# Summing z in linear attention: VectorE pre-adds two of the five key tiles for pairs three to nine

## The chip, the cores and the metric

One core of one Trainium2 chip runs the kernel. The metric is device time in microseconds (us), the median of several runs; a profile of one execution comes with it.

## The reference

A linear attention with exponential features, then a two-layer network. What matters here is the attention, for 8 batches of 8 heads, 576 positions, 64 dimensions, 128 features:

```python
def phi(x):
    proj = np.einsum('bhsd,df->bhsf', x, w_phi)
    proj = proj - np.max(np.abs(proj), axis=-1, keepdims=True)
    return np.concatenate([np.exp(proj), np.exp(-proj)], axis=-1)
q_p, k_p = phi(q), phi(k)
kv = np.einsum('bhsf,bhsd->bhfd', k_p, v)
z = np.sum(k_p, axis=2)
num = np.einsum('bhsf,bhfd->bhsd', q_p, kv)
den = np.einsum('bhsf,bhf->bhs', q_p, z)[..., None] + 1e-06
attn = num / den
h = x @ w_in                       # x: attn as 4608 tokens of 512
out = (max(h, 0) + alpha * min(h, 0)) @ w_out
```

z is the sum of the key features over the 576 positions of one head.

## The kernel before, in words

The work is cut into 32 pairs of heads, numbered from i = 0. A pair's 576 key positions lie on the partitions as five tiles of positions: four of 128 in one buffer (`xk` in the profile, `c["x", 0]` in the code) and the last 64 in another (`k`, `c["x", 1]`), whose other 64 partitions are zero. Per pair, TensorE projects keys and queries (`pj`, `pl`, line 316; chunk 0 is four key tiles, chunk 1 is the fifth key tile and the queries), VectorE takes the row maximum `m` (line 320) and subtracts it (`t`, line 321), ScalarE takes the two exponentials (lines 334 and 329), TensorE sums z with a matrix of ones (`k_z`, line 374) and kv with v (`k_acc`, line 357), ScalarE copies both out (`ks`), TensorE turns them (`kt`) and the queries (`qt`), and then computes the denominators `d` (line 440) and the numerators `n` (line 422).

The reciprocal of the denominators takes a way round: ScalarE copies `d` to `ds`, SyncE's queue writes it as `d9`, VectorE inverts it (`r`, line 459, `invert`), SyncE writes it to memory (`rec_d`, line 462) and reads it back spread over partitions (`rr`, line 467), GpSimd multiplies `s` with it (line 472), and SyncE stores `x_d` (line 475).

Beside this, weights are decoded in blocks, two per visit: SyncE loads `raww` (line 167), ScalarE scales it (`aw`, line 176), VectorE splits it in four instructions (lines 184 to 187, `decode_split`), GpSimd adds (`aw`, line 192), ScalarE casts (`w`, line 127) and GpSimd takes the rest (`w`, line 131). From about 80 us on, the first layer of the network reads attention results back (`xr`, line 528, 1 MB), which ScalarE casts (`xh`) and GpSimd completes (`xl`, line 131).

What is done when is a hand-written list: each step of pair i has a place i + t in `places`, all steps are sorted by place, and TensorE, VectorE, ScalarE and SyncE carry out their own in that order. GpSimd's instructions are put in order by a scheduler. A visit, below, is one turn of this list, from the start of TensorE's sum of z to the next one; it is named by its start in the profile (34.15, 44.73, 55.30 and so on). In the visit that sums z of pair i, VectorE finishes chunk 1 of pair i + 1 and chunk 0 of pair i + 2.

z is formed in two ways. For pairs with i < ZP = 9, `k_sum` does nothing and `k_z` runs over all five tiles; from i = 9 on `k_sum` has VectorE add the five tiles into one in three steps, and `k_z` takes that one. For each tile `k_z` issues four matmuls (two heads, two signs), of 32 columns of ones each, which write four different quarters of the output's partitions; the profile counts two TensorE instructions for each.

Of the kernel before, what the change touches and what calls it, by code (L numbers as in the profile page):

```python
# [8 lines left out]
F32 = mybir.dt.float32  # L9
# [3 lines left out]
ALU = mybir.AluOpType  # L13
# [3 lines left out]
P = 128  # L17
B, H, S, D = 8, 8, 576, 64
FD = 128
# [34 lines left out]
XR_BUFS = 1  # L54
QH_BUFS = 2
ZP = 9


def places(i):
    early = i < ZP  # L60
    end = i >= NPAIR - 2
    return dict(
        ld=-1.90,
        lv=-0.80,
        p=(-0.9955 if early else -0.993, 0.0),
        ke=(-0.26, 0.0011),
        ks=(0.0015, 0.0022, 0.0026),
        kz=1.0002,
        ka=1.0012,
        ko=1.0025,  # L70
        kr=1.10,
        kc=1.16,
        q=(1.34, 1.50, 1.20),
        qe=(1.46, 1.62, 1.28),
        d=2.0004,
        ds=2.0008,
        n=2.005,
        s=2.0055,
        d9=2.25,
        dv=3.0016 if early else 3.20 if end else 2.80,  # L80
        rd=3.0017 if early else 3.21 if end else 2.82,
        rr=3.20 if early else 3.45 if end else 3.001,
        x=3.45 if early else 3.60 if end else 3.20,
        xs=3.90 if early else 3.85 if end else 3.45,
    )
# [27 lines left out]
def fused_kernel(ctx: ExitStack, tc: tile.TileContext, kq, v, w_phi, w_in, w_out, alpha, out):  # L113
    nc = tc.nc
    act, dve, pool, pe = nc.scalar, nc.vector, nc.gpsimd, nc.tensor
# [146 lines left out]
    wk = att.enter_context(tc.tile_pool(name="wk", bufs=3))  # L262
# [18 lines left out]
    def attention_units(i):  # L281
        b, hp = divmod(i, NP)
        c = {}
# [51 lines left out]
            c["x", ch] = x  # L335

        def k_sum(step):
            if i < ZP:
                return
            x = c["x", 0].rearrange("p a h n f -> p (a h) (n f)")  # L340
            if step == 0:
                y = c["y"] = wk.tile([P, 4, 2 * FD], F32, tag="y", name=f"y{i}", bufs=1)
                dve.tensor_tensor(c["y"], x[:, :, : 2 * FD], x[:, :, 2 * FD :], op=ALU.add)
            elif step == 1:
                y = c["y"]
                c["zs"] = wk.tile([P, 4, FD], F32, tag="z", name=f"z{i}", bufs=1)
                dve.tensor_tensor(c["zs"], y[:, :, :FD], y[:, :, FD:], op=ALU.add)
            else:
                z = c["zs"]
                dve.tensor_tensor(z, z, c["x", 1].rearrange("p a h n f -> p (a h) (n f)"), op=ALU.add)  # L350
                c["z"] = z.rearrange("p (a h) f -> p a h f", a=2)
# [12 lines left out]

        def k_z():
            c["kv"] = ps_kv.tile([P, 3, FD], F32, tag="kv", name=f"kv{i}")
            if i < ZP:
                zs = [c["x", 0][:, :, :, j, :] for j in range(4)] + [c["x", 1][:, :, :, 0, :]]
            else:
                zs = [c["z"]]  # L370
            for j, z in enumerate(zs):
                for g in range(4):
                    h, a = divmod(g, 2)
                    pe.matmul(  # L374
                        c["kv"][32 * g : 32 * g + 32, 2],
                        lhsT=ones,
                        rhs=z[:, a, h, :],
                        start=j == 0,
                        stop=j == len(zs) - 1,
                    )  # L380
# [14 lines left out]
        def q_turn(h):  # L395
            pp, tag = (psf, "f") if i < ZP - 1 and h < 2 else (ps_m, "m")
            ps = c["qt", h] = pp.tile([P, 2 if h == 2 else 4, P], F32, tag=tag, name=f"qt{i}_{h}")
            if h == 2:
                for g in range(2):
                    pe.transpose(ps[:, g, :], c["t", 1][:, g, 0, :], ident)  # L400
            else:
                for j in range(4):
                    pe.transpose(ps[:, j, :], c["t", 1][:, h, 1 + j, :], ident)  # L403
# [70 lines left out]
        def store():  # L474
# [5 lines left out]
            (at["lv"], load_v),  # L480
            (at["ka"], k_acc),
            (at["kz"], k_z),
            (at["ko"], kv_out),
            (at["kr"], kv_turn),
# [14 lines left out]
        for n in range(3):  # L499
            us.append((at["ks"][n], lambda n=n: k_sum(n)))  # L500
            us.append((at["q"][n], lambda n=n: q_turn(n)))
            us.append((at["qe"][n], lambda n=n: q_exp(n)))
# [315 lines left out]
```

## Time and profile before

| | us |
|---|---|
| median of 3 runs (1133.55 to 1136.12) | 1135.04 |
| the profiled execution | 1133.75 |
| its span in the profile | 1132.0 |
| TensorE (PE) busy | 1115.9 |
| VectorE (DVE) busy | 634.9 |
| ScalarE (ACT) busy | 560.8 |
| GpSimd (POOL) busy | 215.4 |

Engines are named PE, DVE, ACT, POOL and SP in the rows, and SPq is SyncE's DMA queue. A row of the timeline gives start, duration, engine, line, operation, output and input, and in brackets how long the engine had been idle before and what ended that. The chain is the work that ended last, followed back to the start. DVE's busy share is near 8 tenths in the first tenth of the span, that is where the changed pairs lie.

### The profile page before, as it was taken

To read this page: it belongs to the slowest core of one execution; us is meant where nothing else is said; L and a number is where in the kernel's file an instruction comes from. 1 tells how busy PE (TensorE), PEld (TensorE's weight loads), DVE (VectorE), ACT (ScalarE), POOL (GpSimd) and SP (SyncE) were. 2 spreads that over 40 slices of the span, in tenths; PEclk is the share of its full clock that TensorE was granted. 3 is DMA by queue.
4 is the path that set the end of the run, shared out by engine and by line. 5 is a ranking of instruction groups with operands and counts; after the bars stand their busy time and mean duration, and the time that the engine had idled before them with its cause. 6 is when DMAs were issued, how large, how long until landed. Compare 5 with 4: busy or idle time off the path is not lost.

```text
span 1132.0 us, 18386 instructions
## 1 busy us (share of the span) xinstructions
PE 1115.9 (99%) x7246; PEld 868.6 (77%) x7246; DVE 634.9 (56%) x979; ACT 560.8 (50%) x1149; POOL 215.4 (19%) x219
## 2 busy tenths in 40 slices
PE   8999999999999999999999999999999999999998
PEld 6766777777777777677678888888888888888886
DVE  7888858698788777745862432424243423333323
ACT  5777665666676665664543342424333333333332
POOL 1345332423324242243542000000000000000000
PEclk9999999999999999999999999999999999999999
DMA  5466264546546364466616130303030302020021
GB/s 192 149 189 207 77 201 156 185 135 210 174 140 190 109 215 153 147 218 211 221 66 232 47 112 1 112 1 112 1 112 1 112 0 85 28 82 30 4 71 38
DMA packets 74245, 133.68 MB, mean 118 GB/s; under 512 B 14640, under 2 KB 24752, under 8 KB 73520
## 3 DMA queue, kind: packets, MB, share of 16 engines
q1 hardware_dynamic: 71856, 122.48, 33.5%
q0 software_dynamic: 2016, 9.96, 2.6%
q8 instruction: 57, 0.93, 0.3%
q14 instruction: 28, 0.23, 0.1%
q10 hardware_dynamic: 288, 0.07, 0.0%
HBM read 93.92 MB, written 38.42 MB: 117 GB/s over the span
## 4 chain that ended last, share of the span: by engine, by line
PE 90%; DVE 5%; ACT 2%; DMA 1%; issue 1%; POOL 1%; ACTq 0%; DVEq 0%; SPq 0%
PE h L512 11%; PE h L514 11%; PE h L513 11%; PE po L520 8%; PE po L518 8%; PE po L519 8%; PE kv L357 6%; PE pj L316 5%; PE n L422 5%; PE o L518 4%; PE o L520 4%; PE o L519 3%; PE d L440 2%; PE qt L403 2%; PE kv L374 1%; DVE m L320 1%
## 5 line engine op out<-in xcount | busy, mean ns | idle before, releaser
L243 DVE SCALAR_TENSOR_TENSOR g<-r,aln,g 128x512 f32<-128x512 f32 x144 | 112.8, 783 | 318.6 <-ACT g L239 318.2
L238 ACT ACTIVATE r<-h 128x512 f32<-128x512 f32 x144 | 86.7, 602 | 286.5 <-PE h L514 286.4
L131 DVE TENSOR_TENSOR gl<-g,gh 128x512 fp32r<-128x512 f32 x144 | 104.6, 726 | 84.8 <-ACT gh L127 84.3
L127 ACT CAST gh<-g 128x512 fp32r<-128x512 f32 x144 | 90.1, 626 | 94.3 <-DVE g L243 94.3
L239 ACT ACTIVATE g<-h 128x512 f32<-128x512 f32 x144 | 85.9, 597 | 2.5 <-DMA part_d<-os 2.5
L320 DVE TENSOR_REDUCE m<-pj 128x8 f32<-128x1024 f32 (+1 forms) x66 | 78.2, 1185 | 12.8 <-PE pj L316 12.6
L520 PE MATMUL po<-gl,wd 128*128 128x512 f32 x216 | 84.3, 390 | 0.0
L518 PE MATMUL po<-gh,wd 128*128 128x512 f32 x216 | 84.3, 390 | 0.0
L519 PE MATMUL po<-gh,wd 128*128 128x512 f32 x216 | 84.3, 390 | 0.0
L192 POOL TENSOR_TENSOR aw<-ew,aw 128x256 f32<-128x256 f32 x64 | 56.0, 875 | 129.4 <-DVE ew L187 127.9
L316 PE MATMUL pj<-w_sb,raw 64*128 64x128 f32 x1024 | 73.4, 283 | 7.0 <-DVE t L321 6.1
L316 PEld LDWEIGHTS pj<-w_sb,raw 64*128 64x128 f32 x1024 | 64.0, 191 | 21.0 <-issue 13.7
L321 DVE TENSOR_TENSOR t<-pj,m 128x1024 f32<-128x1024 f32 (+1 forms) x66 | 78.7, 1192 | 2.3
L518 PE MATMUL o<-gh,w 128*128 128x512 f32 x180 | 76.1, 423 | 0.2
L512 PE MATMUL h<-xh,w 128*128 128x512 f32 x180 | 75.8, 421 | 0.0
L472 POOL TENSOR_TENSOR s<-s,rr 128x576 f32<-128x576 f32 x32 | 48.1, 1502 | 143.9 <-DMA rr<-rec_d 111.0
L514 PE MATMUL h<-xl,w 128*128 128x512 f32 x180 | 70.9, 394 | 1.9 <-POOL xl L131 1.9
L520 PE MATMUL o<-gl,w 128*128 128x512 f32 x180 | 71.2, 396 | 1.5 <-DVE gl L131 1.3
L413 ACT ACTIVATE qf<-qt 128x512 f32<-128x512 f32 x128 | 68.5, 615 | 6.3 <-PE qt L403 6.3
L519 PE MATMUL o<-gh,w 128*128 128x512 f32 x180 | 70.6, 392 | 0.0
L513 PE MATMUL h<-xh,w 128*128 128x512 f32 x180 | 70.5, 392 | 0.0
L518 PE MATMUL po<-gh,w 128*128 128x512 f32 x180 | 70.2, 390 | 0.0
(108 smaller groups left out, 2409.4 us busy)
## 6 DMA issues: line engine op xcount, KB each, us to landing
xr<-x_d SPq DMA_DIRECT2D x18, 1024.0 KB
raw<-kq_dram SPq DMA_DIRECT2D x31, 576.0 KB
v<-v_dram SPq DMA_DIRECT2D x32, 320.0 KB
w_d<-raww SPq DMA_DIRECT2D x38, 256.0 KB
rr<-rec_d SPq DMA_DIRECT2D x64, 144.0 KB
x_d<-s SPq DMA_DIRECT2D x32, 288.0 KB
part_d<-os SPq DMA_DIRECT2D x36, 256.0 KB
pt<-part_d SPq DMA_DIRECT2D x9, 1024.0 KB
```

The costliest lines, as they stand in the source:

```text
L127: return act.copy(dst, src)
L131: return eng.tensor_tensor(dst, src, f(hi), op=ALU.subtract)
L238: act.activation(st["r"], ps, AF.Relu, scale=-1.0)
L243: dve.scalar_tensor_tensor(g, st["r"], aln[:, ff : ff + 1], g, op0=ALU.mult, op1=ALU.add)
L316: pe.matmul(dst[h, j], lhsT=c["raw"][hs, ts], rhs=w_sb[hs], start=True, stop=True)
L320: dve.tensor_reduce(m, src, axis=AX.X, op=ALU.max, apply_absolute_value=True)
L512: pe.matmul(ps, lhsT=wt[0][:, ws], rhs=xh, start=n == 0, stop=False)
L513: pe.matmul(ps, lhsT=wt[1][:, ws], rhs=xh, start=False, stop=False)
L514: pe.matmul(ps, lhsT=wt[0][:, ws], rhs=xl, start=False, stop=n == NK - 1)
L518: pe.matmul(ps, lhsT=wt[2][:, ws], rhs=gh, start=first, stop=False)
L519: pe.matmul(ps, lhsT=wt[3][:, ws], rhs=gh, start=False, stop=False)
L520: pe.matmul(ps, lhsT=wt[2][:, ws], rhs=gl, start=False, stop=last)
```

## The change

For the pairs with 2 <= i < 9, `k_sum` now runs at its first step: VectorE adds tiles 0 and 1 of the pair's exponentials into a tile `z` of 128 x 512 (four groups of 128). `k_z` then sums tiles 2 and 3, the fifth tile, and this sum: four tiles in place of five. The pairs 0, 1 and those from 9 on are as before. The buffer `z` was there before, for the later pairs.

```diff
+ZY = 2
...
         def k_sum(step):
-            if i < ZP:
+            if i < ZY or i < ZP and step > 0:
                 return
             x = c["x", 0].rearrange("p a h n f -> p (a h) (n f)")
-            if step == 0:
+            if i < ZP:
+                c["zs"] = wk.tile([P, 4, FD], F32, tag="z", name=f"z{i}", bufs=1)
+                dve.tensor_tensor(c["zs"], x[:, :, :FD], x[:, :, FD : 2 * FD], op=ALU.add)
+            elif step == 0:
...
         def k_z():
             c["kv"] = ps_kv.tile([P, 3, FD], F32, tag="kv", name=f"kv{i}")
-            if i < ZP:
+            if ZY <= i < ZP:
+                zs = [c["x", 0][:, :, :, j, :] for j in (2, 3)] + [c["x", 1][:, :, :, 0, :]]
+                zs.append(c["zs"].rearrange("p (a h) f -> p a h f", a=2))
+            elif i < ZP:
```

Lines of the changed file stand 1 to 7 higher than those before (line 374 is 381, line 459 is 466). On VectorE, the work of pair 4 in the visit at 44.73: before,

```order
L320 TENSOR_REDUCE m_1_2_683<-pj_1_666 128x8
L321 TENSOR_TENSOR t_1_663<-pj_1_666,m_1_2_683 128x2x512
L459 RECIPROCAL r_1_730<-d_1_622 128x9
L184 TENSOR_SCALAR aw_0_0_657<-aw_0_0_657 128x256
L185 SCALAR_TENSOR_TENSOR aw_0_0_657<-raww_0_0_629,aw_0_0_657 128x256
```

and now

```order
L321 TENSOR_REDUCE m_1_2_683<-pj_1_666 128x8
L322 TENSOR_TENSOR t_1_663<-pj_1_666,m_1_2_683 128x2x512
L344 TENSOR_TENSOR z_726<-xk_654 128x512
L466 RECIPROCAL r_1_728<-d_1_622 128x9
L185 TENSOR_SCALAR aw_0_0_657<-aw_0_0_657 128x256
L186 SCALAR_TENSOR_TENSOR aw_0_0_657<-raww_0_0_629,aw_0_0_657 128x256
L187 TENSOR_SCALAR ew_0_0_733<-aw_0_0_657 128x256
L188 SCALAR_TENSOR_TENSOR ew_0_0_733<-raww_0_0_629,ew_0_0_733 128x256
L321 TENSOR_REDUCE m_0_0_748<-pj_0_739 128x8
```

The added instruction stands between chunk 1's subtraction and the reciprocal of pair 1's denominators, and with it the decoding split and the next projection's maximum stand one place later. On TensorE, z of the same pair, one visit later: before,

```order
L374 MATMUL kv_848<-xk_654,ones 32x128 x16
L374 MATMUL kv_848<-k_0_130,ones 32x128 x4
L440 MATMUL d_869<-qf_788,sf_774 32x288 x8
L357 MATMUL kv_848<-xk_654,v_620 64x256 x8
L357 MATMUL kv_848<-k_0_130,v_620 64x256 x2
```

and now

```order
L381 MATMUL kv_846<-xk_654,ones 32x128 x8
L381 MATMUL kv_846<-k_0_130,ones 32x128 x4
L381 MATMUL kv_846<-z_726,ones 32x128 x4
L447 MATMUL d_863<-qf_786,sf_772 32x288 x8
L361 MATMUL kv_846<-xk_654,v_620 64x256 x8
L361 MATMUL kv_846<-k_0_130,v_620 64x256 x2
```

Sixteen matmuls in place of twenty, the last four of them on the new sum. The orders of ScalarE and SyncE are the same in both kernels. On GpSimd the scheduler exchanged two rows, in the visit at 87.03 (`s` is pair 4's result, `w` and `aw` the decoding): before,

```order
L131 TENSOR_TENSOR w_89<-aw_1_256_1110,w_89 128x256
L192 TENSOR_TENSOR aw_1_0_1143<-ew_1_0_1221,aw_1_0_1143 128x256
L472 TENSOR_TENSOR s_1087<-s_1087,rr_1264 128x576
L131 TENSOR_TENSOR w_90<-aw_1_0_1143,w_90 128x256
L131 TENSOR_TENSOR xl_0_1288<-xr_0_1252,xh_0_1287 128x512
```

and now

```order
L132 TENSOR_TENSOR w_89<-aw_1_256_1104,w_89 128x256
L193 TENSOR_TENSOR aw_1_0_1137<-ew_1_0_1213,aw_1_0_1137 128x256
L132 TENSOR_TENSOR w_90<-aw_1_0_1137,w_90 128x256
L479 TENSOR_TENSOR s_1081<-s_1081,rr_1256 128x576
L132 TENSOR_TENSOR xl_0_1280<-xr_0_1244,xh_0_1279 128x512
```

The decoding's `w` stands ahead of `s` there; this is the one exchange in GpSimd's order.

## Rows read from the trace of the kernel before

**Rows 1.** The page, busy time by engine (share of the span) and instructions.
```profile
PE 1115.9 (99%) x7246; PEld 868.6 (77%) x7246; DVE 634.9 (56%) x979; ACT 560.8 (50%) x1149; POOL 215.4 (19%) x219
```

**Rows 2.** Stretches, one per visit: length, busy us per engine, clock, DMA share, GB/s.
```profile
44.73:55.30 10.57, 10.57 (x143) 7.48 (x142) 9.04 (x18) 8.21 (x21) 4.28 (x5) 1.00 0.67 193
55.30:65.88 10.58, 10.58 (x144) 7.49 (x142) 8.96 (x18) 8.12 (x21) 4.46 (x5) 1.00 0.71 214
...
87.03:99.90 12.87, 11.30 (x144) 7.67 (x142) 11.36 (x18) 10.81 (x26) 7.16 (x8) 1.00 0.78 226
```

**Rows 3.** The chain that ended last: start, duration, z over five tiles and over one.
```profile
55.37 1.23 PE kv L374 x40
...
117.31 0.35 PE kv L374 x8
```

**Rows 4.** Tile z: DVE's additions of 128x512 for the later pairs, ns min/median/max.
```profile
L347 DVE TENSOR_TENSOR z<-y x23: 691/693/1714, 106.3 to 478.4; 128x512 f32<-128x512 f32 x23
```

**Rows 5.** The timeline of the visit at 55.30, all engines.
```profile
56.03 1.43 POOL L472 TENSOR_TENSOR s<-s,rr 128x576 f32<-128x576 f32 x1 [4.83 <-DMA rr<-rec_d]
...
57.74 1.22 DVE L321 TENSOR_TENSOR t<-pj,m 128x1024 f32<-128x1024 f32 x1
58.10 0.74 POOL L192 TENSOR_TENSOR aw<-ew,aw 128x256 f32<-128x256 f32 x1
...
58.89 0.20 DVE L459 RECIPROCAL r<-d 128x9 f32<-128x9 f32 x1
...
59.36 0.92 POOL L131 TENSOR_TENSOR w<-aw,w 128x256 fp32r<-128x256 f32 x1 [0.52 <-ACT w L127]
...
59.80 0.63 DVE L186 TENSOR_SCALAR ew<-aw 128x256 uint32<-128x256 uint32 x1
...
60.10 0.46 ACT L384 COPY ks<-kv 128x384 f32<-128x384 f32 x1
...
61.02 1.23 DVE L320 TENSOR_REDUCE m<-pj 128x8 f32<-128x1024 f32 x1
...
62.28 1.23 DVE L321 TENSOR_TENSOR t<-pj,m 128x1024 f32<-128x1024 f32 x1
...
62.99 0.55 PE L389 MATMUL kt<-ident,ks 128*128 128x128 f32 x3
...
64.51 0.29 DVE L184 TENSOR_SCALAR aw<-aw 128x256 uint32<-128x256 uint32 x1 [1.01 <-ACT aw L176]
...
64.89 1.06 PE L316 MATMUL pj<-w_sb,raw 64*128 64x128 f32 x16
```

**Rows 6.** The timeline, 91.9 to 95.5: VectorE's split beside GpSimd.
```profile
91.92 1.43 DVE L184 TENSOR_SCALAR aw<-aw 128x256 uint32<-128x256 uint32 x1 [1.02 <-ACT aw L176]
91.92 1.28 POOL L131 TENSOR_TENSOR xl<-xr,xh 128x512 fp32r<-128x512 f32 x1
...
93.15 0.78 POOL L192 TENSOR_TENSOR aw<-ew,aw 128x256 f32<-128x256 f32 x1
...
93.38 0.83 DVE L185 SCALAR_TENSOR_TENSOR aw<-raww,aw 128x256 uint32<-128x256 uint32 x1
```

**Rows 7.** The timeline of the visit at 76.45, from the reciprocal on.
```profile
80.04 0.20 DVE L459 RECIPROCAL r<-d 128x9 f32<-128x9 f32 x1
...
80.27 0.33 SPq L462 DMA_DIRECT2D rec_d<-r  x1
...
80.83 0.38 SPq L528 DMA_DIRECT2D xr<-x_d  x1
```

**Rows 8.** The chain that ended last, 86 to 99 us: start, duration, what.
```profile
86.06 5.21 DMA raww<-w_out_dram
...
91.36 0.46 ACT aw L176
...
98.81 1.16 PE pj L316 x16
```

## The prediction

> **What bounds the kernel now.** I read the page first: PE is busy 99% of the span [rows 1], so only what shortens PE's list, or opens or closes a hole in it, can move the time. Then I cut the changed stretch into its visits. In six visits in a row, from 23.57 to 87.03, PE has no hole at all: 10.57 or 10.58 us long and as much PE busy, at full granted clock, with DVE at about 9.0 us [rows 2]. Only the visit at 87.03 is longer, 12.87 us with 11.30 of PE, a hole of 1.57. So in the six visits a PE instruction less is worth its time as long as DVE keeps up, and DVE has some 1.6 us of room per visit. The third view is the chain across the longer visit: it leaves PE, waits for a load of weights to land (86.06 to 91.27), goes through ACT at 91.36 and DVE's split, and is back on PE at 98.81 [rows 8]. The last view is the timeline of an ordinary visit [rows 5], which tells how much late DVE work PE forgives.
>
> **The change part by part.** *PE.* z over five tiles takes 1.23 us for 40 instructions, over one tile 0.35 us for 8 [rows 3]: (1.23 - 0.35) / 32 = 0.0275 us per instruction. One tile less is 8 instructions, 0.22 us for each of seven pairs, 1.54 us in all, falling in the visits at 34.15 to 99.90. PE's new wait for the sum costs nothing: the sum is made a visit (10 us) earlier. Nothing further down is waiting for an absolute time, so what is won or lost by 100 us stays.
>
> *DVE.* Each pair gains an addition of 128x512. The later pairs' additions of this shape have a median of 0.693 us [rows 4]; 4.9 us in seven. It stands after t of chunk 1, which ends at 58.96 in the visit shown, ahead of the reciprocal, the split and the next m and t, which end at 62.28 + 1.23 = 63.51. PE needs that t at 64.89 [rows 5]. The cover is 1.38 us, 1.16 once PE is 0.22 earlier: 0.69 alone is hidden. Behind t, DVE was idle 1.01 until 64.51 anyway, so nothing piles up from visit to visit. The total also fits: 8.96 + 0.69 = 9.65 in a visit of 10.36.
>
> *What stands behind the addition.* The reciprocal moves too, and with it everything on SP's queue that waits behind it: rec_d, raw, rr, v, d9 and two loads of raww. raw and v are needed about a visit later, I cost them at nothing. But rr releases POOL: s started at 56.03 after 4.83 us of idling for it, and s, w and aw run back to back until 58.84, only 0.12 us before t ends [rows 5]. With the reciprocal 0.69 late, rr and this trio come that much later in the next visit, and then aw runs just when the addition wants to start.
>
> *What a meeting costs.* Rows show that DVE stands still while POOL's instruction runs: at 91.92 a DVE instruction that takes 0.29 at 64.51 took 1.43 beside a POOL one of 1.28, and at 93.38 one with two inputs ended (94.21) only after POOL's aw of 93.15 + 0.78 = 93.93 [rows 5, 6]. In the visit shown one of the split's four took 0.63 in place of some 0.29, beside w. The Trainium skill says why ("SBUF — State Buffer", section "SBUF: two separate sides"): a DVE instruction with two SBUF inputs and a GpSimd instruction that reads SBUF take a shared pair of ports for a whole instruction, and the other blocks. By that rule the addition, whose inputs both lie in SBUF, waits for whatever POOL has running; without it the sum would be that of the first rival below. The rows on the split agree with it; no row of the kernel before shows this very addition beside POOL.
>
> No row prices the addition's meetings, so I bound them. The addition's wait lies between 0 and one POOL instruction of 0.74; the split behind it then meets aw or w, between 0 and another 0.74. I take half for the addition, 0.37, since its start falls anywhere in aw, and a whole one, 0.74, for the split, because POOL's aw and w now come after the addition, as at 91.92, where POOL and DVE took turns. Then t of the next chunk is late by 0.69 + 0.37 + 0.74 = 1.80, against a cover of 1.16: PE loses 0.64 per visit. The visits at 23.57 and 34.15 have no s yet and lose nothing. At 44.73 the trio is late for the first time; I take half, 0.32. At 55.30 and 65.88 I take 0.64 each. Together 1.60; the ends are 0 and three times 0.69 + 0.74 + 0.74 - 1.16 = 1.01, 3.03.
>
> *ACT.* Its cast waits for POOL's aw, and queued behind it are ds, the exponentials of k's last tile and ks. ks ended at 60.56 and PE turns it at 62.99 [rows 5]: 2.4 us of cover against about 1 of delay, so nothing; without that cover kt would be late by the rest.
>
> *The hole at 87.03.* Its cause lies one visit earlier. The reciprocal at 80.04 lets SP go to rec_d at 80.27 and to xr, 1 MB, at 80.83 [rows 7]. The DMA engines are then busy (share 0.78 over the visit [rows 2]) until raww lands, at 91.27; ACT, which is in order, scales it at 91.36, and DVE, whose m and t stand behind the split, lets PE go at 98.81 [rows 8]. So the end of the hole follows the reciprocal, not PE. What PE wins in the visits at 76.45 and 87.03 is lost in the hole, and what DVE costs there is hidden in it. The reciprocal comes with the visits' own shift, and later in its visit by 0.69 + 0.37 = 1.06. In the visit itself DVE idles 1.02 before the split, which takes the eighth pair's addition; the exchange on POOL takes one w of about 0.7 out from between s and xl, a help of at most that size that I set against this addition.
>
> *The sum.* PE's four savings before that reciprocal (34.15 to 65.88): -0.88. PE's waits for DVE: +1.60. The reciprocal's own lateness: +1.06. PE's saving after the hole: -0.22. Together +1.56 us. The profiled execution, 1133.75 us with a span of 1132.0, would become 1135.3. The median of the runs stands 1.29 above it, at 1135.04, and becomes **1136.6 us**: 0.14% slower, below 0.2% (2.27 us), which is about what a measurement of this kernel can tell from no change.
>
> **The rivals.** *The cover holds.* POOL's trio and the addition miss each other, so DVE's 0.69 is hidden. Then -0.88 + 0.69 - 0.22 = -0.41: 1134.6 us. For it: the idle DVE time of 1.01 and the room of 1.6 per visit. Against: 0.12 us between trio and addition, and a trio that is released by what the addition delays.
>
> *The full gain.* The hole does not follow the reciprocal, because raww's landing is set by something else: -1.54, 1133.5 us. A little more could come from the exchange on POOL, up to 0.7 of the hole. Against it speaks ACT's waiting for that landing.
>
> *Slower, by turns of POOL and DVE.* Each meeting costs a whole POOL instruction, for the addition as for the split. Then PE waits 1.01 in each of three visits, the reciprocal at 80.04 is late by 0.69 + 0.74 = 1.43, and the sum is -0.88 + 3.03 + 1.43 - 0.22 = +3.36: 1138.4 us, 0.3% slower. It decides as soon as the trio is more than about 0.5 late, so that aw has only begun when t ends; the lateness of one visit's reciprocal is the next visit's trio, so it feeds itself. The Trainium skill's lock (the same page and section) lets nothing share: by it alone this rival, and not the middle, is the outcome. The rows agree as far as the split goes.
>
> That the change doesn't do what it says is ruled out by the order of the instructions: four matmuls fewer and one addition more in each of seven pairs.
>
> **How the numbers follow.** The forecast (part of the meetings, +0.3 to +2.6) has 0.48, the slower rival 0.24, the cover that holds 0.22, the full gain 0.06. The range takes in the full gain at its lower end, 1133.5, and at its upper the slower rival with some 0.5 for a third meeting, 1138.9; what is left out is a gain from the exchange and meetings in every visit. The forecast's own range is 1135.3 to 1137.6. Slower by over 0.2% (above 1137.3): most of the slower rival, 0.22, and 0.11 of the forecast's upper end, 0.33. Faster by over 0.2% (below 1132.8): the upper part of the full gain, 0.04. The rest, 0.63, is no change.
>
> **What would show it.** Right: PE's z takes about 1.01 us for 32 instructions in the seven pairs; DVE's additions last more than 0.69 in the visits from 44.73 on; PE waits for t before its second projection there; the xr load starts later against PE than before, and PE's hole ahead of 100 us is longer than 1.57. Wrong: additions of 0.69 throughout and visits of 10.36, which would be the first rival; or a hole that has shrunk by what PE won, the second. If DVE's additions were short and PE still lost time, the fault would lie with SP's queue alone.

## The result, and the profile after

The change takes 1137.07 us (median of 20 runs, 1134.49 to 1139.96) where the kernel before takes 1134.24 (20 runs): a ratio of 1.0024, 95% interval 1.0017 to 1.0032. Timed once more beside other kernels (e7 below) it is 1136.82 against 1134.59: 1.0015 [1.0002, 1.0028]. So it costs some 2 to 3 us, about as much as a measurement can tell from no change. The forecast was 1136.6, inside a range of 1133.5 to 1138.9; it was counted from a median of 3 runs, 1135.04, so as a difference it was 1.56 against 2.83 and 2.23 measured.

The busy times of the page, beside [rows 1]:

```profile
PE 1117.5 (98%) x7190; PEld 868.9 (76%) x7190; DVE 642.3 (57%) x986; ACT 560.2 (49%) x1149; POOL 214.7 (19%) x219
```

TensorE has 56 instructions less, as it should, and VectorE seven more, but VectorE's busy time has grown by 7.4 us and not by seven times 0.69. The chain that ended last has z over four tiles (the sum is the fourth) in 1.01 us where [rows 3] had 1.23 for five, and the load that ends PE's hole, which took 5.21 in [rows 8]:

```profile
55.34 1.01 PE kv L381 x32
...
85.97 6.63 DMA raww<-w_out_dram
```

The stretches of three visits, from z to z, beside [rows 2] (length first, then busy us of PE, PEld, DVE, ACT and POOL, the granted clock, and DMA):

```profile
44.71:55.27 10.56, 10.56 (x136) 7.33 (x134) 10.07 (x19) 8.32 (x21) 4.70 (x5) 1.00 0.70 204
...
76.15:87.12 10.97, 10.62 (x136) 7.33 (x134) 10.56 (x17) 7.16 (x18) 5.42 (x6) 1.00 0.69 224
87.12:101.30 14.18, 11.42 (x136) 7.40 (x134) 12.95 (x20) 11.31 (x26) 6.71 (x6) 1.00 0.76 230
```

A visit without a loss would be 10.58 - 0.22 = 10.36, and the one at 34.35 is that. The three from 44.71 on are 10.56, 10.42 and 10.46, the one at 76.15 is 10.97, DVE is at 9.9 to 10.6 us where it was at 9, and the visit with the hole has grown from 12.87 to 14.18. Where the time goes stands in the timeline (start, duration, engine, line; in brackets the idle time before and what ended it):

```profile
27.67 0.68 DVE L344 TENSOR_TENSOR z<-xk 128x512 f32<-128x512 f32 x1
...
48.00 0.75 POOL L132 TENSOR_TENSOR w<-aw,w 128x256 fp32r<-128x256 f32 x1
48.29 1.00 DVE L344 TENSOR_TENSOR z<-xk 128x512 f32<-128x512 f32 x1
48.69 1.19 POOL L193 TENSOR_TENSOR aw<-ew,aw 128x256 f32<-128x256 f32 x1
...
58.88 0.73 POOL L193 TENSOR_TENSOR aw<-ew,aw 128x256 f32<-128x256 f32 x1
59.00 1.16 DVE L344 TENSOR_TENSOR z<-xk 128x512 f32<-128x512 f32 x1
...
79.88 1.26 DVE L344 TENSOR_TENSOR z<-xk 128x512 f32<-128x512 f32 x1
...
81.06 0.20 DVE L466 RECIPROCAL r<-d 128x9 f32<-128x9 f32 x1
...
82.35 0.38 SPq L535 DMA_DIRECT2D xr<-x_d  x1
...
86.03 1.16 PE L317 MATMUL pj<-w_sb,raw 64*128 64x128 f32 x16 [0.35 <-DVE t L322]
...
92.02 1.44 DVE L344 TENSOR_TENSOR z<-xk 128x512 f32<-128x512 f32 x1 [0.67 <-ACT xk L335]
...
97.10 0.55 PE L396 MATMUL kt<-ident,ks 128*128 128x128 f32 x3 [0.93 <-ACT ks L391]
100.21 1.16 PE L317 MATMUL pj<-w_sb,raw 64*128 64x128 f32 x16 [1.05 <-DVE t L322]
```

The addition meets POOL as feared: at 59.00 it takes 1.16 and ends 0.55 after POOL's aw (59.61); at 48.29 it starts inside POOL's w, which ends at 48.75, and takes 1.00, and POOL's aw, which starts inside the addition, takes 1.19 in place of 0.73. The first addition, at 27.67, where POOL has nothing to do, takes 0.68. The reciprocal of [rows 7] comes at 81.06, xr at 82.35, and the projection that ended the hole at 98.81 [rows 8] comes at 100.21.

**How lags are read below.** Executions don't start alike: VectorE's t of pair 2 stands at 21.20 before and at 21.39 here. All times of other kernels in the table and the texts on it are taken less that difference. "Lag" is then how much later the same ScalarE instruction (the first layer's r, read from the h in PSUM) stands than in the kernel before: at 134 us 135.25 - 134.09 - 0.19 = 0.97 for the change, 1.99 at 505, 4.00 at the end. Medians are over the runs, everything else is from one profile each.

| kernel | median, before beside it | ratio [95%] | reciprocal | after the hole | lag at 134 | grows 452 to 505 | lag at the end |
|---|---|---|---|---|---|---|---|
| before | | | 80.04 | 98.81 | | | |
| the change | 1137.07, 1134.24 | 1.0024 [1.0017, 1.0032] | 80.87 | 100.02 | 0.97 | 0.95 | 4.00 |
| e7 the change again | 1136.82, 1134.59 | 1.0015 [1.0002, 1.0028] | 81.06 | 100.69 | 1.66 | 0.97 | 2.61 |
| e1 add behind the reciprocal | 1134.11, 1133.40 | 1.0007 [0.9996, 1.0017] | 79.94 | 98.95 | -0.01 | 0.29 | 0.22 |
| e2 add in the idle gap | 1135.37, 1133.40 | 1.0013 [1.0004, 1.0022] | 79.17 | 99.00 | 0.93 | 0.45 | 3.41 |
| e3 PE's half | 1134.27, 1133.40 | 1.0007 [0.9997, 1.0016] | 79.16 | 97.94 | -1.10 | 0.18 | 1.03 |
| e4 VectorE's half | 1136.45, 1133.40 | 1.0023 [1.0012, 1.0034] | 81.23 | 100.15 | 1.33 | 0.00 | 0.96 |
| e5 reduction in its place | 1135.76, 1134.59 | 1.0005 [0.9994, 1.0016] | 79.80 | 98.59 | -0.25 | 1.40 | 3.43 |
| e6 before, late reciprocal | 1146.33, 1134.59 | 1.0095 [1.0076, 1.0113] | 88.43 | 106.03 | 11.53 | 0.01 | 10.24 |
| e8 change, xr later | 1137.10, 1134.59 | 1.0011 [0.9998, 1.0024] | 80.23 | 96.76 | 2.24 | 0.57 | 3.41 |
| e11 e8, casts later | 1135.42, 1134.26 | 1.0011 [1.0000, 1.0022] | 80.48 | 97.35 | 0.20 | 0.59 | 0.62 |
| e12 e11 and e1 | 1133.93, 1134.26 | 0.9999 [0.9987, 1.0011] | 79.18 | 95.91 | -1.63 | 0.47 | -1.52 |
| e13 before, with e11's rows | 1135.22, 1134.26 | 1.0009 [0.9996, 1.0023] | 80.05 | 100.70 | 2.85 | -0.01 | 4.35 |
| e14 change, padded code | 1147.64, 1134.65 | 1.0119 [1.0100, 1.0139] | 81.32 | 100.00 | 0.96 | 0.00 | 0.54 |

### The profile page after: what moved, and what is told of

Read it like the earlier page. It is cut to its first block, busy times and chain, and to the rows that moved or that the text cites. A ratio compares the mean times of both kernels' runs of the same rounds, so it can differ in the third digit from the quotient of the medians.

```text
span 1136.2 us, 18288 instructions
## 1 busy us (share of the span) xinstructions
PE 1117.5 (98%) x7190; PEld 868.9 (76%) x7190; DVE 642.3 (57%) x986; ACT 560.2 (49%) x1149; POOL 214.7 (19%) x219
## 4 chain that ended last, share of the span: by engine, by line
PE 89%; DVE 6%; ACT 2%; issue 1%; DMA 1%; POOL 1%; SPq 0%; DVEq 0%; ACTq 0%
PE h L519 11%; PE h L521 11%; PE h L520 11%; PE po L525 8%; PE po L527 8%; PE po L526 8%; PE kv L361 5%; PE pj L317 5%; PE n L429 5%; PE o L525 3%; PE o L527 3%; PE o L526 3%; PE d L447 2%; PE qt L410 2%; DVE m L321 1%; PE kv L381 1%
```

## The experiments

### Where the addition stands (e1, e2)

Two kernels do all the work of the change and move the addition alone: behind the reciprocal, and into the gap in which VectorE waits for ScalarE's aw.

```diff
-        ks=(0.0015, 0.0022, 0.0026),
+        ks=(0.0030 if early else 0.0015, 0.0022, 0.0026),
```

and, for e2, `0.3000` in place of `0.0030`.

> The changed kernel with the addition one place later on VectorE: behind the reciprocal, still ahead of the split. Lateness theory (the addition costs because it delays the reciprocal, and with it SyncE's queue, GpSimd's trio and the load of xr): the reciprocal is on time, GpSimd's trio ends before the addition again, the hole of PE ahead of 100 us is about as long as before the change; -1.1 to +0.3 us against the kernel before. Room theory (VectorE has no room for seven more additions, wherever they stand): like the change, +2 to +4 us. GpSimd theory (the exchange of two rows in GpSimd's order costs it; this kernel has the order of before): 0 to -1.5 us, with additions as long as in the change (about 1.16 us).

Measured: the reciprocal is back where it was (79.94), the hole ends at 98.95, the lag at 134 us is nothing, and the median is 0.7 us above before, less than can be told. So in this profile the change costs nothing on balance up to 134 us when the reciprocal doesn't stand behind the additions; the median's interval overlaps that of the change's second timing (e7). e1 moves more than the reciprocal: GpSimd's order is that of the kernel before again, and the additions, 0.63 to 1.30, took 0.63 in four visits of seven, where POOL's w, if it came during one, took 0.80 to 1.12, so that POOL waited and not VectorE. One meeting in this profile costs PE more, in the visit at 65 us, where the split meets POOL's s:

```profile
65.12 1.42 POOL L479 TENSOR_TENSOR s<-s,rr 128x576 f32<-128x576 f32 x1 [2.97 <-issue]
65.13 1.71 DVE L188 SCALAR_TENSOR_TENSOR ew<-raww,ew 128x256 f32<-128x256 uint32 x1
...
70.30 0.63 DVE L344 TENSOR_TENSOR z<-xk 128x512 f32<-128x512 f32 x1
70.37 1.16 PE L317 MATMUL pj<-w_sb,raw 64*128 64x128 f32 x16 [0.70 <-PE kv L361]
```

The instruction that takes 0.42 alone takes 1.71 and PE loses 0.7; the other visits between 34.24 and the hole are 10.35 or 10.36.

> The changed kernel with the addition still later: behind chunk 0's subtraction and ahead of the second split, where VectorE was idle for about 1.0 us per visit. Lateness theory: additions of 0.69 us, visits of 10.36 us, reciprocal, trio and xr earlier by what PE won, so that the hole comes earlier too: -1.1 us (-0.8 to -1.6). Room theory: +1 us or more. GpSimd theory: like the first kernel of this call.

In the gap the addition meets nobody: 0.68 in six visits out of seven, visits of 10.36, the reciprocal 0.87 early. And yet the hole ends at 99.00, no earlier than before: raww's scaling begins at 91.26 (91.36 before), 11.4 us after xr instead of 10.5, and the split behind it starts only when POOL's w ends (here the profile's own times, 0.36 earlier):

```profile
90.89 0.45 ACT L177 ACTIVATE aw<-raww 128x256 f32<-128x256 f32 x1 [1.05 <-DMA raww<-w_out_dram]
91.07 0.73 POOL L132 TENSOR_TENSOR w<-aw,w 128x256 fp32r<-128x256 f32 x1
...
91.80 1.39 DVE L185 TENSOR_SCALAR aw<-aw 128x256 uint32<-128x256 uint32 x1 [2.40 <-POOL w L132]
```

The last addition, 1.86 beside POOL's s, comes at 98.50, too late to hold up that projection. The lag is 0.93 at 134 us, and the median is 2.0 above before, where 1.1 below was expected: the forecast missed. So an earlier reciprocal isn't passed on in full. The medians of e1 and e2 lie within each other's intervals; at 134 us only e1 has no lag. Why raww landed late is not settled; most of the lag at the end of this profile comes at 550 us, with the clock (below).

### The two halves (e3, e4)

e3 has PE's part alone: no addition, and z sums tiles 1, 2, 3 and the fifth, so tile 0 is missing from z. e4 has VectorE's part alone: the addition is made and read by nobody, and z sums five tiles.

```diff
 # e3
-            if i < ZY or i < ZP and step > 0:
+            if i < ZP:
...
-                zs = [c["x", 0][:, :, :, j, :] for j in (2, 3)] + [c["x", 1][:, :, :, 0, :]]
-                zs.append(c["zs"].rearrange("p (a h) f -> p a h f", a=2))
+                zs = [c["x", 0][:, :, :, j, :] for j in (1, 2, 3)] + [c["x", 1][:, :, :, 0, :]]
 # e4
-            if ZY <= i < ZP:
+            if False:
```

> TensorE's half alone: for the seven pairs z is summed from four tiles and nothing is added on VectorE; z leaves out the first tile there. Lateness theory: PE's saving of 0.22 per pair is kept up to the reciprocal at 80 and behind the hole: -1.1 us (-0.8 to -1.6). If the hole is tied to something that doesn't move with PE (the rival by which the hole swallows whatever comes before it): -0.2 us, that is no change.

> VectorE's half alone: the addition is made where the change makes it, nobody reads it, and TensorE sums all five tiles. Lateness theory: the cost of the change without its saving: +2 to +4 us, the additions from 45 us on longer than 0.69 us, xr about 1 to 2 us later than before. GpSimd theory (here GpSimd's order is that of before): within 0.5 us of before. Additive check: this one and the half on TensorE should make up the change, 2.83 us.

PE's half gives visits of 10.36 and a lead of 1.10 at 134 us, of 1.54 that were taken out; by the end of this profile it has lost all of it, 1.45 of it at 550 us, and the median isn't below before's. VectorE's half costs as much as the whole change (1.0023). The medians of the halves stand 0.87 and 3.05 above before's, together 3.9 where the change has 2.83 and 2.23; each interval is some 2 us wide, so this neither shows nor refutes that they add up. In VectorE's half the visits are 10.57 to 10.72, so in them the cover of 1.38 us nearly holds; what it costs is in the reciprocal, 1.19 late, and in the hole behind it, which ends 1.34 late:

```profile
80.72 1.16 DVE L344 TENSOR_TENSOR z<-xk 128x512 f32<-128x512 f32 x1
81.80 0.20 DVE L466 RECIPROCAL r<-d 128x9 f32<-128x9 f32 x1
...
100.73 0.49 PE L317 MATMUL pj<-w_sb,raw 64*128 64x128 f32 x4 [1.05 <-DVE t L322]
```

GpSimd's order in e4 is that of the kernel before, and in e5 below it is that of the change, so the exchange of w and s isn't what costs.

### Length or meeting (e5)

In place of the addition VectorE takes a maximum over the same two tiles, as long but with one input; z leaves out tile 0.

```diff
-                dve.tensor_tensor(c["zs"], x[:, :, :FD], x[:, :, FD : 2 * FD], op=ALU.add)
+                dve.tensor_reduce(rz, x[:, :, :FD], axis=AX.X, op=ALU.max)
```

(`rz` is 128 x 4; z's tiles as in e3.)

> In place of the addition VectorE takes a maximum over tiles 0 and 1 (one SBUF input, the same 128 x 512), which nobody reads; z is summed over four tiles and leaves tile 0 out. TensorE has the change's savings; VectorE has as many instructions as in the change, but this one has a single input. Theory of meetings (the change's addition takes 1.0 to 1.44 us beside POOL instead of 0.68, and hands that lateness to the reciprocal): the reduction takes 0.6 to 0.7 us in every visit, POOL's aw beside it takes its usual 0.73 instead of 1.18, the reciprocal ahead of the 1 MB load comes at 80.2 to 80.7 instead of 81.06, the projection after the hole at 99.0 to 99.5 instead of 100.21, and the median is 1 us or so below the change's, 1135 to 1136. Theory of plain length (any 0.7 us of VectorE ahead of the reciprocal costs the same): reciprocal at 81.0, projection at 100.0 or later, median 1136.5 to 1137.5. Theory that the cost is not in VectorE's place at all: median as e3, 1134.3.

```profile
57.87 0.73 POOL L193 TENSOR_TENSOR aw<-ew,aw 128x256 f32<-128x256 f32 x1
58.12 0.68 DVE L344 TENSOR_REDUCE rz<-xk 128x4 f32<-128x512 f32 x1
...
79.47 0.20 DVE L465 RECIPROCAL r<-d 128x9 f32<-128x9 f32 x1
```

All seven reductions take 0.67 to 0.69, six of them beside POOL, POOL's aw beside them 0.73, the visits 10.35 to 10.40. The reciprocal comes a little earlier than before (79.80) and the projection after the hole too (98.59): a lead of 0.25 at 134 us, where the change has a lag of 0.97 and 1.66. So 0.68 us of VectorE in this place is paid by PE's savings, and what the change loses in this stretch, 1.2 to 1.9 us, comes from the meetings. The Trainium skill says ("SBUF — State Buffer", section "SBUF: two separate sides") that a VectorE instruction with two SBUF inputs blocks a GpSimd one that reads SBUF, and the other way round. The additions at 48.29 and 59.00 above agree with it; the reduction, with one input, meets the same aw, and neither is longer. It also writes far less than the addition, 128x4, which no run here tells apart. The median, 1135.76, is higher than this stretch explains; the last of these sections takes that up.

### The reciprocal alone (e6)

The kernel before, with the reciprocal behind the first split, and no other work.

```diff
-        dv=3.0016 if early else 3.20 if end else 2.80,
-        rd=3.0017 if early else 3.21 if end else 2.82,
+        dv=3.00441 if early else 3.20 if end else 2.80,
+        rd=3.00442 if early else 3.21 if end else 2.82,
```

> The kernel before, with no addition at all, but with the reciprocal of the early pairs moved behind the first split's four instructions, where an addition and a half would push it. Theory of the reciprocal's lateness: the visits up to 87 keep 10.57, the reciprocal ahead of the 1 MB load comes 1.4 to 2.0 later than 80.04, the projection after the hole 1.0 to 2.0 later than 98.81, and nothing gives it back: median +1 to +2 over before, 1134.5 to 1135.5. Theory of room on VectorE (it is the additional work that costs): no work is added, so the hole ends at 98.8 and the median is before's within 0.5. Rival: rr comes so late that POOL's s stands beside the next chunk's work in every visit, and PE waits for t in the visits themselves: visits over 10.8 and a median over 1136.

It costs 11 us, far more than the theories gave; the rival had named visits over 10.8, which came, for another reason. The rows show a ring that the expectation had missed:

```profile
49.94 0.44 ACT L176 ACTIVATE aw<-raww 128x256 f32<-128x256 f32 x1 [2.15 <-DMA raww<-w_in_dram]
...
50.48 0.52 DVE L184 TENSOR_SCALAR aw<-aw 128x256 uint32<-128x256 uint32 x1 [2.02 <-ACT aw L176]
...
53.06 0.20 DVE L459 RECIPROCAL r<-d 128x9 f32<-128x9 f32 x1
...
57.99 0.94 SPq L167 DMA_DIRECT2D raww<-w_in_dram  x2
...
62.02 0.44 ACT L176 ACTIVATE aw<-raww 128x256 f32<-128x256 f32 x1 [2.78 <-DMA raww<-w_in_dram]
```

The split waits for ACT's aw, that for raww, raww stands on SP's queue behind rec_d, rec_d waits for the reciprocal, and now the reciprocal stands behind the split. The reciprocals stand at 53.06, 64.99, 76.72 and 88.50, 11.7 to 11.9 apart, and the four visits from 44.79 on are 11.25 to 12.41. That SP's queue hangs on the reciprocal is shown by it more sharply than by anything else; the size says nothing about 0.8 us of lateness, since in the change the reciprocal stays ahead of the split.

### The hole (e8, e11, e12, e13)

If the hole ends with raww because 1 MB stands ahead of it, xr can go behind the first raww of its visit. Its casts, on ScalarE, go later with it.

```diff
-FX0 = (1.80, 1.35, 0.95, 0.45)
+FX0 = (1.30, 1.05, 0.80, 0.45)
...
-FL0 = 2.20
+FL0 = 1.55
```

> The change, with the first 1 MB load (xr) issued behind the first raww load of its visit instead of right behind rec_d, and its four casts placed later (FL0 = 1.55 for 2.20; FX0 = 1.30, 1.05, 0.80, 0.45 for 1.80, 1.35, 0.95, 0.45). All arithmetic is done. Theory of the hole (PE's hole ahead of 100 us ends with raww's landing, which stands behind 1 MB that the reciprocal releases): raww lands by about 88 instead of 92.6, ACT scales it in its turn, and the hole of 2.5 us or so goes; what is left of it is DVE's own lateness. Projection after it 2 to 2.5 us earlier, at 97.7 to 98.2, median 1134.5 to 1135. Theory that the hole is only moved: xr then lands later, POOL's xl and the first layer's start wait for it, and 0 to 0.5 us is won in all. Rival: the traffic collides with the next raw and rr loads, so that a later visit has the hole: median as the change's or above, 1137 to 1139.

The projection comes at 96.76, 3.3 us earlier than in the change. Ten microseconds on, PE waits again:

```profile
99.89 1.41 POOL L479 TENSOR_TENSOR s<-s,rr 128x576 f32<-128x576 f32 x1 [4.88 <-DMA rr<-rec_d]
...
105.85 0.72 POOL L193 TENSOR_TENSOR aw<-ew,aw 128x256 f32<-128x256 f32 x1
...
106.60 0.41 ACT L128 CAST w<-aw 128x256 fp32r<-128x256 f32 x1 [3.85 <-POOL aw L193]
...
108.34 0.55 PE L396 MATMUL kt<-ident,ks 128*128 128x128 f32 x3 [2.25 <-ACT ks L391]
```

POOL's aw stands behind s, two xl and w, ScalarE's w waits 3.85 for it, and behind that w stands the ks that PE wants. Then the granted clock is 0.81 over 110 to 116, matmuls of 0.39 take 0.63 until 112, and all is given back: the lag at 134 us is 2.24, and the median, 1137.10, is the change's, as the rival had it. e11 casts later still (`FX0 = (1.30, 0.60, 0.40, 0.20)`), which puts that aw ahead of two xl; e12 is e11 with e1's row; e13 is the kernel before with e11's two rows.

> The change with the first xr behind the visit's first raww (FL0 = 1.55) as in e8, and the last three of its casts later still (FX0 = 1.30, 0.60, 0.40, 0.20), so that GpSimd's order has the decoding's aw of 98 us ahead of two xl instead of behind s, xl, w and xl. Theory: e8 lost the won 2.6 us only because ACT's w, and with it ks, waited 3.85 us for that aw; with it ahead, ks is there by 105 to 106, PE's hole of 2.25 at 106 goes, the granted clock stays at 1.00 there, and this run stands 1 to 2 us ahead of the kernel before at 134 us; median 1132.5 to 1134. Rival (something between 100 and 134 us waits for an absolute time, the rr load or the xl chain): the hole comes again, at another instruction, +1 to +2.2 at 134 us, median 1136 to 1137.

> As e11, with the addition behind the reciprocal as in e1. If the reciprocal's lateness and the hole are the two things that eat TensorE's savings, this has both away and shows the seven savings of 0.22 and the hole: 2 to 3 us ahead of before at 134 us, median 1131.5 to 1133, below e11 by 0.5 to 1.2. If only the hole matters, it equals e11 within 0.4. If neither, it stands at before or above.

> The kernel before (no addition, five tiles) with the same two rows of the table as e11. It tells how much of e11 and e12 is the transfer's place alone. Theory: the hole of 1.57 in the visit at 87.03 goes, the projection after it comes at 97.3 instead of 98.81, 0.5 to 1.5 us ahead at 134 us, median 1132.5 to 1134; e12 then is 0.7 to 1.5 below it (seven savings of 0.22 that are no longer eaten), and e11 within 0.7 of it on either side. Rival (the visits' savings don't pay even without the hole): e12 is not below this one.

In e11 that aw comes at 102.06, ks at 104.81, and the wait of 2.25 is gone, but PE waits 1.42 for ks before, at 95.73, and 1.72 for an xl behind:

```profile
111.41 0.50 PE L521 MATMUL h<-xl,w 128*128 128x512 f32 x1 [1.72 <-POOL xl L132]
```

It keeps a lag of 0.20 at 134 us, against 0.97 and 1.66, between what its theory and its rival expected. e12, with both moves, leads by 1.63 there, less than the 2 to 3 expected, and by 1.52 at the end, the only one that still leads there; its median is equal to before's (0.9999) and 1.3 and 1.5 below those of e13 and e11, and the intervals overlap. e13 was expected 0.5 to 1.5 ahead and lags by 2.85: moving xr is no gain by itself. Its ScalarE reaches the first cast before xr has landed and waits 4.19, PE waits for ks, and the granted clock is 0.68 over 100 to 104:

```profile
95.08 0.62 ACT L127 CAST xh<-xr 128x512 fp32r<-128x512 f32 x1 [4.19 <-DMA xr<-x_d]
...
97.03 0.55 PE L389 MATMUL kt<-ident,ks 128*128 128x128 f32 x3 [2.15 <-ACT ks L384]
```

So PE's hole is not one load. raww, xr, rr and the xl on POOL all arrive within these 20 us, and taking one out of the way brings up the next. None of these kernels beats the one before by more than can be told.

### Once more, and the late microsecond (e7, e14)

> The changed kernel once more, for a second profile of it. If what the first profile shows from 452 us on (+1 us at 452 to 505, +2 us at 534 to 556, where TensorE's granted clock falls to 0.78) belongs to the change, it stands here too, at the same places: +4 us at the end. If it belongs to single executions, this profile has +1.0 to +1.2 up to 134 us, as the first, and a different rest: anything from +1 to +4 at the end, and the granted clock at 550 to 558 may be 1.00.

The second profile has the same 0.97 between 452 and 505 us and not the 2.1 between 534 and 556. So the first is of the change; the second need not come with it. The granted clock falls there in e2, e3 and e5 too (0.66, 0.57 and 0.66 over the same 4 us) and stays at 1.00 in the other ten profiles, and the lags at the end of e2, e3 and e5 hold 1.4 to 2.0 from it; whether some of the kernels make it likelier can't be told from one or two profiles each. In the change, PE's hole at 550 us is the same as in its repeat, but the granted clock behind it isn't (clock, the third number from the end; the change, then its repeat):

```profile
550.00:554.00 4.00, 2.71 (x7) 1.93 (x8) 2.65 (x4) 1.31 (x3) 4.00 (x7) 0.78 0.44 116
```

```profile
550.00:554.00 4.00, 2.82 (x12) 2.00 (x13) 2.76 (x4) 1.49 (x3) 4.00 (x6) 1.00 0.46 115
```

The 0.97 is this: VectorE's split, in the kernel before,

```profile
454.98 0.32 SPq L462 DMA_DIRECT2D rec_d<-r  x1
457.01 1.11 SPq L467 DMA_DIRECT2D rr<-rec_d  x2
460.92 1.40 POOL L472 TENSOR_TENSOR s<-s,rr 128x576 f32<-128x576 f32 x1 [5.39 <-issue]
462.51 0.28 DVE L184 TENSOR_SCALAR aw<-aw 128x256 uint32<-128x256 uint32 x1
```

and in the change:

```profile
456.20 0.32 SPq L469 DMA_DIRECT2D rec_d<-r  x1
459.70 1.11 SPq L474 DMA_DIRECT2D rr<-rec_d  x2
463.42 1.41 POOL L479 TENSOR_TENSOR s<-s,rr 128x576 f32<-128x576 f32 x1 [6.67 <-DMA rr<-rec_d]
463.72 1.25 DVE L185 TENSOR_SCALAR aw<-aw 128x256 uint32<-128x256 uint32 x1
...
473.12 0.49 PE L525 MATMUL o<-gh,w 128*128 128x512 f32 x1 [0.91 <-ACT gh L128]
```

rr is issued 3.50 us after rec_d instead of 2.03. So s runs just when the split begins, the split takes 1.25 instead of 0.28, the first layer's product behind it (gh, cast by ScalarE) is late, and PE waits 0.91 for it. Over all kernels up to here this interval goes with one thing: 2.0 to 2.2 us where z takes five tiles (before, e4, e6, e13), 2.9 to 3.5 where it takes four (the change, its repeat, e1, e2, e3, e5, e8, e11, e12). What is lost goes with the split's first instruction: 0.18 in e3, where it takes 0.48, 0.29 in e1 with 0.58, 0.57 in e8 with 0.85, 0.95 in the change with 1.25, nothing where it takes 0.28. In e5, with 0.79, the 1.40 holds another wait as well, 0.57 of PE for ScalarE's ds at 459.69. The pairs in question are done by 120 us; what is left of the difference at 450 is that TensorE's program is shorter. The instruction queue of the DMA shows it: each of its 57 packets brings 0.93 MB / 57 = 16 KB of program, one for some 127 of TensorE's 7246 instructions; before, one comes between 448 and 449 us, with five tiles in e4 between 450 and 451, in the change between 457 and 458, between rec_d and rr. (Queue, packets, MB, share of the 16 engines, in the microsecond from 457.)

```profile
q8 instruction: 1, 0.02, 8.9%
```

e14 puts the 56 instructions back at the start of the kernel, in the warm-up.

```diff
-NWARM = 7
+NWARM = 35
...
-        pe.matmul(ps_w[:, 0], lhsT=warm, rhs=warm, start=True, stop=True)
+        pe.matmul(ps_w[:, 0, :24], lhsT=warm, rhs=warm[:, :24], start=True, stop=True)
```

> The change, with 35 warm-up matmuls of 24 columns at the start in place of 7 of 128, so that TensorE has as many instructions again as before (the change took 56 out, as many as 28 matmuls count). All arithmetic is done. The question is the second late loss, 0.95 and 0.97 us between 452 and 505 us in two profiles of the change. There an instruction load (one packet of 16 KB on the instruction queue) lies at 457 us, between rec_d and rr, in the kernels whose z takes four tiles; in those with five tiles it lies at 448 to 450. rec_d to rr is 3.50 and 3.27 us in the change, 2.9 to 3.1 in the others with four tiles, 2.0 to 2.2 with five. Theory of the code's place: with the instructions back, the load lies at 448 to 452, rec_d to rr is 2.0 to 2.3 us, GpSimd's s no longer meets the split (0.28 in place of 1.25), PE does not wait for gh at 473, and the lag does not grow between 452 and 505 us (under 0.2); the median is about 1 us below the change's, 1135.5 to 1136.3. Theory that the lag of the early stretch itself makes it (another phase against other transfers): nothing of this changes, 3.2 to 3.5 us, split 1.2, lag +0.9, median 1136.8 to 1137.2. The early stretch (lag of 1 to 1.7 us at 134 us) is expected to stay in both.

```profile
468.24 0.32 SPq L469 DMA_DIRECT2D rec_d<-r  x1
470.18 1.11 SPq L474 DMA_DIRECT2D rr<-rec_d  x2
...
475.76 0.28 DVE L185 TENSOR_SCALAR aw<-aw 128x256 uint32<-128x256 uint32 x1
```

The warm-up got far longer than I meant it to, 15.13 us in place of 3.36, and the whole run starts 11.99 later; so the median stands 1.0 above before's once that is taken off (1147.64 - 11.99 = 1135.65 against 1134.65). The lag still answers the question: the packet comes between 461 and 462, over 6 us ahead of rec_d, rec_d to rr is 1.94, the split 0.28, and the lag grows by 0.00 between 452 and 505 us, with the early stretch as in the change (0.96 at 134 us). What exactly the packet holds up, rec_d's write or what SP waits for behind it, the rows don't show.

## Why the prediction was right, and where not

**PE's savings: right.** 0.22 per pair, z in 1.01 us, visits of 10.36 where nothing waits (e2, e3, e12).

**PE's waits for DVE: mechanism right, size too large.** The prediction had 1.60 in the three visits from 44.73 to 65.88. Their lengths above 10.36 make 0.20 + 0.06 + 0.10 = 0.36. The visit at 76.15 loses another 0.61, which the prediction had counted as hidden in the hole, so the four lose 0.97; in e7 they lose 0.96, all of it in the first three. The term was 0.6 of what was set: of the price of a meeting, 0.37 for the addition was near (1.00 to 1.26 against 0.68, so 0.32 to 0.58), but 0.74 for each split behind it was too much; behind the addition at 59.00, one of its instructions took 0.83 in place of 0.42, the others their usual time. Of the three rows on which the prediction rested the blocking, only the one at 93.38 has two SBUF inputs; those at 91.92 and 59.80 have one, so they show a stall, but not by the rule on two inputs that it named.

**The reciprocal's lateness: right within its visit.** Forecast 1.06; from the start of the visit it comes 81.06 - 76.15 = 4.91 in the change and 80.86 - 76.35 = 4.51 in e7, against 80.04 - 76.45 = 3.59 before, so 1.32 and 0.92 late. The end of the hole, forecast -0.88 + 1.60 + 1.06 = 1.78 late, is 1.21 and 1.88 late in the two profiles; after the last saving of 0.22, forecast 1.56, the lag is 0.97 and 1.66. This nearness is in part luck: the reciprocal itself came only 0.83 and 1.02 late and not 1.78, and from it to the end of the hole another 0.38 and 0.86 were lost, which the prediction didn't have. That the hole follows the reciprocal holds for most kernels in which only VectorE or PE was changed: 18.77 to 19.15 us from one to the other in before, the change, e1, e3, e4 and e5, with the reciprocal anywhere from 79.16 to 81.23. In e2 and e7 it is 19.83 and 19.63: in e7 the last addition, ahead of the split in the visit of the hole, took 1.87; in e2 the split waited for POOL's w, as shown above. The prediction had hidden that addition in idle time of VectorE: in the change it started only when ScalarE's xk was there and took 1.44 beside POOL's s, and the split, with raww's aw ready at 93.14, started at 93.50.

**"Nothing further down is waiting for an absolute time": wrong.** This was the step that let the sum stop at 100 us. Another 0.95 is lost at 460 to 473 us, by POOL's s meeting the split, because 56 instructions less shift the point at which the next 16 KB of program is loaded. With it the sum would have been 1.56 + 0.95 = 2.5, the size that the medians show (2.8 and 2.2); the two profiles lag by 1.99 and 3.06 at 505 us. The forecast of 1136.6 was near, then, by luck as well: with a term for waits that was too large, two that were missing, and a kernel before that was taken 0.8 too slow from 3 runs.

**The rivals.** The cover that holds (-0.41) fell, though e4 shows that it nearly holds within the visits; it fell by the reciprocal. The full gain fell: even e3, which makes no addition, leads by 1.10 and not 1.54 at 134 us, and its median isn't faster. Slower by whole turns of POOL (+3.36, 1138.4) has the right mechanism and too high a price: in the visits from 48 to 80 us the addition was 0.32 to 0.58 longer in the change and 0.05 to 0.56 in e7, not 0.74, since one that starts inside a POOL instruction waits only for what is left of it, and both medians lie below that time, between it and the forecast. The exchange on POOL, set against the eighth addition, plays no part that e4 can show.

## What to carry to other kernels

Before work is put on an engine that has room, look at what stands behind it in its order: here the small reciprocal behind the addition releases a DMA queue, and moving the addition right behind it took the cost of that stretch away (no lag at 134 us in place of 0.97 and 1.66), while moving it further back left 0.93. The addition with two SBUF inputs cost more than its length beside GpSimd (up to 1.87 in place of 0.68); a reduction with one cost only its length here. And when differences of a microsecond are compared, keep the number of instructions equal: 56 fewer moved a load of the program from 448 to 457 us, and that cost 0.95.

## What the runs showed of the hardware that was not expected

- A VectorE reduction with one SBUF input took 0.67 to 0.69 us in all seven visits, six of them beside POOL, an addition over the same data 0.68 where POOL had nothing to do (once in each profile of the change) and 0.73 to 1.87 in the other twelve cases, ten of them 1.00 or more. But one input is no safe sign: the split's first instruction has one, and took 1.25 at 463.72 beside s, in place of 0.28. The Trainium skill names a second case beside two SBUF inputs, a VectorE instruction in a 2-port mode ("SBUF — State Buffer", section "SBUF: two separate sides"); no run here shows in which mode the split runs.
- A packet of 16 KB on the instruction queue, between rec_d and rr, goes with 0.9 to 1.5 us more between the two; e14 moved it away, and the interval was 1.94.
- After the same wait of PE for POOL's xl at 550 us, with pauses of 0.69 and 1.17, the granted clock was 0.78 from 550 to 554 us in one execution of the change and 1.00 in the other: matmuls of 0.39 took 0.63, which is the level of 1.2 GHz for part of the stretch. It fell behind pauses of 0.65 to 0.69 and 1.18 to 1.19 in e2, e3 and e5 too (0.66, 0.57, 0.66), and not behind those of 0.68 to 0.69 and 1.17 to 1.19 in the kernel before, e1, e8 and e12. What decides it was not tried.
- 28 more warm-up matmuls made the warm-up longer by 11.8 us: with 24 columns each instruction took 15.13 / 70 = 0.216, with 128 columns 3.36 / 14 = 0.240, at a granted clock of 1.00 in both. At the start, narrow matmuls on full weights are nearly as dear as wide ones.
